# Remainder products of two blocks at once, a one-row bias, one-operation masks and merged placing copies in a gated attention and MLP decode kernel

## The chip, the cores and the metric

The kernel runs on one core of a Trainium2 chip. The metric is the time of one execution on the device, in microseconds, as the median of several runs; the profile is of one further execution, and its span is about 1.2 us shorter than the time of that run. A program on one core can be told apart only as fast or not fast by its distance from the fastest run of the same kernel.

Engines: PE multiplies matrices (PEld is the loading of its weights), DVE is VectorE, ACT is ScalarE, POOL is GpSimd, SP (SyncE) issues nearly all DMA transfers. A load lands when its last bytes have arrived. The granted clock is the share of its full clock that PE was allowed in a stretch of time.

## The reference, cut to what matters

One decode step for 8 sequences: an attention over a sliding window of 2048 positions (32 query heads, 16 key/value heads of 128), a two-layer MLP on a layer norm, and a gate that mixes the two.

```python
x = A_x                                                  # (8, 1, 576)
g = sigmoid((x * gate_w).sum(-1, keepdims=True))
q = x @ wq                                               # 576 -> 32 heads x 128
scores = einsum(q, k[last 2048]) * 128 ** -0.5           # k, v: 8 x 16 x 2048 x 128 bf16 each
a = (softmax(scores) @ v) @ wo                           # 4096 -> 576
b = gelu(layernorm(x) @ w1 + b1) @ w2 + b2               # 576 -> 4608 -> 576
out = g * a + (1 - g) * b
```

K and V are 67 MB each and all weights together 20 MB: 154 MB must come in.

## The kernel before

A small planner lists all operations with their dependences and an assumed cost, orders them for each engine, and puts semaphores in. SP issues the loads in one fixed order. K comes in 16 loads of 4.19 MB into two buffers, V in 32 loads of 2.10 MB into five, which w1 and later w2 share. A load waits, in SP's order, until its buffer is free. Each K unit is transposed twice by DVE and multiplied by PE; after four units two softmaxes follow, and V products use the result.

The parts that the change touches:

```python
# masks, DVE
o_own0 = add("dve", lambda e: e.memset(view("own"), 0.0), ...)
o_own = [add("dve", ... e.memset(own[32*a:32*a+32, a:a+1], 1.0) ...) for a in range(4)]
o_i20 = add("dve", lambda e: e.memset(view("i2"), 0.0), ...)
o_i2 = [add("dve", ... e.tensor_copy(i2[32*q:32*q+32, :, q//2, :], ident[block q]) ...) for q in range(4)]
for q in range(4):
    o_i32.append(add("dve", ... e.tensor_copy(i32[32*q:32*q+32, :], ident[block q]) ...))
...
# wq: 576 rows are 4 x 128 and a remainder of 64; two halves of the columns share the 128 rows of wq_r
for hq in range(Hq):                                     # 32 blocks of 128 columns
    out_ = ps[:, BK_Q, hq*8: hq*8+8]
    for t in range(4):
        e.matmul(out_, wq_m[:, t, block hq], xT[:, t, :], start=(t == 0), stop=False)
    c = hq % 16
    e.matmul(out_, wq_r[:, block c], xT[:, 4 + hq//16, :], start=False, stop=True)
...  # w1 the same: 36 blocks of 4 + 1 products, weights read with a step of 9 columns
# softmax of a group, DVE: the maxima of three row groups copied beside the first's, then
m01 = max(MX, GA); m23 = max(GB_, GC_); tt = max(m01, m23)
...
# placing: quadrant copies of the attention output into the layout that wo's products want
if i == NUQ - 9:
    place(slice(0, 8), slice(0, 6), list(oT_done.values()))
elif i >= NUQ - 8:                                       # after each two of the last eight V units
    c = (i % 8) // 2
    place_done[c] = place(slice(c, 8, 4), slice(6, 8), [oT_done[i-1], oT_done[i]])   # 16 copies
...
# bias of the second layer, loaded into 8 rows, multiplied by 1 - g on the diagonal
d = dma("sp", lambda e: e.dma_start(b2_sb, B_b2.partition_broadcast(8)), ...)
# the loads: each waits for its buffer, in SP's order
d = dma("sp", load, "s%d" % s, 32*512*Dh*2, deps=slot_free[s] + slot_free[s+1], after=last_dma[-1:])
```

## Time and profile before

| | before |
|---|---|
| time, median (three runs) | 366.19 us (366.12 to 366.73) |
| span of the profiled run | 364.9 us |
| DMA | 154.58 MB, 424 GB/s over the span, 90% or more busy in 39 of 40 slices |
| PE, DVE busy | 239.4 us (66%), 226.5 us (62%) |
| end of the last load to the end of the span | 362.2 to 364.9 us |

The page's slices and the chain of waits are shown in the prediction. First the chain's shares by engine, on which rival 1 of the prediction rests:

```profile
DMA 62%; DVE 24%; PE 11%; issue 1%; SPq 0%; DVEq 0%
```

Second the timeline (start us, length us, engine and line, what, count) where wq's products run, one L474 product per group of five being a remainder:

```profile
18.34 0.25 PE L472 MATMUL ps<-arena 128*128 128x8 bf16 x4
18.45 0.17 PE L474 MATMUL ps<-arena 128*128 128x8 bf16 x1
```

Third the timeline near the end: the last V unit's products (L711), the last 16 placing copies (L761), and two of PE's waits for pieces of w2.

```profile
350.07 1.90 PE L711 MATMUL ps<-arena 128*32 128x512 bf16 x16 [1.11 <-DMA arena<-in_A_v_cache_dram]
...
354.06 3.03 DVE L761 COPY arena<-arena 32x4 bf16<-32x4 bf16 x16
...
359.39 1.64 PE L555 MATMUL ps<-arena 128*8 128x288 bf16 x24 [1.35 <-DMA arena<-in_B_w_dram]
361.52 0.53 PE L555 MATMUL ps<-arena 128*8 128x288 bf16 x6 [0.49 <-DMA arena<-in_B_w_dram]
```

The brackets give the idle time of the engine just before, and what ended it. PE stands waiting for w2 at the end.

### The profile page before, as it was taken

What the parts mean: (1) busy time and instruction counts of PE and PEld (TensorE: products, weight loads), DVE (VectorE), ACT (ScalarE), POOL (GpSimd) and SP (SyncE); (2) the same over time, 40 slices, a digit from 0 to 9 for tenths busy, and PEclk for the clock granted to TensorE, in tenths of its full rate; (3) what the DMA queues carried; (4) which work ended last, traced back from release to release, by engine and by line L of the source; (5) the groups of instructions that cost most, each with busy time, mean ns of one, the idle gap of its engine ahead of it and who ended that gap; (6) DMA issues with size and microseconds to landing.
All of it is one profiled execution on the core that took longest, in us unless ns stands there. A gap on an engine that the chain in (4) does not pass through costs nothing.

```text
span 364.9 us, 3980 instructions
## 1 busy us (share of the span) xinstructions
PE 239.4 (66%) x1679; PEld 115.0 (32%) x1679; DVE 226.5 (62%) x340; ACT 22.4 (6%) x53; POOL 17.4 (5%) x80
## 2 busy tenths in 40 slices
PE   0269684838498938274959484738959297577575
PEld 0159331312143414022423232214424133234232
DVE  4700995675999280759965362789781739777221
ACT  1010000000000000000100000001100000001000
POOL 5021000001000000010000000000000000000000
PEclk9999998778589969596996978676978796859899
DMA  9999999999999999999999999999999999999995
GB/s 376 435 404 451 406 451 411 451 432 415 445 426 443 420 436 431 424 438 424 436 426 440 422 442 420 439 422 438 424 436 444 426 410 436 425 431 429 431 425 222
DMA packets 9690, 154.58 MB, mean 424 GB/s; under 512 B 1052, under 2 KB 1220, under 8 KB 2888
## 3 DMA queue, kind: packets, MB, share of 16 engines
q1 hardware_dynamic: 9616, 154.29, 98.9%
q8 instruction: 13, 0.21, 0.2%
q10 hardware_dynamic: 56, 0.03, 0.0%
q14 instruction: 5, 0.04, 0.0%
HBM read 154.31 MB, written 0.01 MB: 423 GB/s over the span
## 4 chain that ended last, share of the span: by engine, by line
DMA 62%; DVE 24%; PE 11%; issue 1%; SPq 0%; DVEq 0%
DMA arena<-in_A_k_cache_dram 54%; DVE arena L666 18%; PE ps L678 6%; DMA arena<-in_A_v_cache_dram 5%; PE ps L711 4%; DMA arena<-in_B_w_dram 4%; DVE arena L639 3%; DVE arena L597 1%; DVE arena L631 1%; DVE arena L600 0%; DVE arena L606 0%; PE ps L612 0%; DVE arena L614 0%; PE ps L555 0%; SPq L798 0%
## 5 line engine op out<-in xcount | busy, mean ns | idle before, releaser
L666 DVE STREAM_TRANSPOSE arena<-arena 128x4096 f32<-128x4096 f32 x32 | 140.7, 4424 | 85.4 <-DMA arena<-in_A_k_cache_dram 85.0
L678 PE MATMUL ps<-arena 128*32 128x512 bf16 x512 | 141.7, 440 | 62.7 <-DVE arena L666 62.7
L678 PEld LDWEIGHTS ps<-arena 128*32 128x32 bf16 x512 | 52.3, 105 | 144.7 <-DVE arena L666 67.7
L711 PE MATMUL ps<-arena 128*32 128x512 bf16 x512 | 60.7, 453 | 23.8 <-DVE arena L602 18.6
L711 PEld LDWEIGHTS ps<-arena 128*32 128x32 bf16 x512 | 24.8, 110 | 50.4 <-issue 31.7
L639 DVE STREAM_TRANSPOSE arena<-arena 128x512 bf16<-128x512 bf16 x32 | 30.8, 1019 | 0.0
L728 PE MATMUL ps<-arena 128*128 128x16 f32 x128 | 17.0, 264 | 5.6 <-ACT arena L722 3.9
L761 DVE COPY arena<-arena 32x4 bf16<-32x4 bf16 (+1 forms) x80 | 12.9, 161 | 10.1 <-POOL arena L749 7.9
L728 PEld LDWEIGHTS ps<-arena 128*128 128x128 f32 x128 | 15.5, 191 | 11.5 <-ACT arena L722 9.6
L722 ACT ACTIVATE arena<-ps 128x512 f32<-128x512 f32 x16 | 9.6, 598 | 148.9 <-PE ps L711 148.9
L749 POOL TENSOR_TENSOR arena<-arena 128x8 bf16<-128x8 f32 x30 | 5.9, 231 | 229.9 <-ACT arena L738 229.9
L597 DVE TENSOR_REDUCE arena<-ps 128x1 f32<-128x512 f32 x8 | 5.5, 692 | 12.2 <-PE ps L678 12.1
L510 PE MATMUL ps<-arena 128*128 128x8 bf16 x144 | 10.9, 201 | 2.6 <-DMA arena<-in_B_w_dram 2.6
L608 ACT ACTIVATE arena<-ps,arena 128x512 bf16<-128x512 f32 x8 | 5.5, 687 | 107.4 <-DVE arena L606 107.4
L510 PEld LDWEIGHTS ps<-arena 128*128 128x128 bf16 x144 | 10.8, 157 | 3.1 <-DMA arena<-in_B_w_dram 3.1
L555 PE MATMUL ps<-arena 128*8 128x288 bf16 (+1 forms) x140 | 9.3, 288 | 3.6 <-DMA arena<-in_B_w_dram 3.4
L659 POOL TENSOR_TENSOR arena<-arena 128x32 bf16<-128x32 bf16 x32 | 6.5, 240 | 86.0 <-PE ps L678 76.9
L612 PE MATMUL ps<-arena 128*128 128x32 f32 x16 | 3.9, 328 | 8.6 <-DVE arena L611 8.6
L631 DVE TENSOR_SCALAR arena<-arena 128x512 bf16<-128x512 bf16 x32 | 9.0, 324 | 0.0
L425 PE MATMUL ps<-arena 8*128 8x8 bf16 x8 | 0.6, 170 | 11.0 <-DVE arena L398 7.0
L512 PE MATMUL ps<-arena 128*128 128x8 bf16 x36 | 7.2, 201 | 0.0
L555 PEld LDWEIGHTS ps<-arena 128*8 128x8 bf16 (+1 forms) x140 | 4.6, 85 | 7.8 <-DMA arena<-in_B_w_dram 4.9
(84 smaller groups left out, 77.8 us busy)
## 6 DMA issues: line engine op xcount, KB each, us to landing
arena<-in_A_k_cache_dram SPq DMA_DIRECT2D x16, 4096.0 KB, 25.2
arena<-in_A_v_cache_dram SPq DMA_DIRECT2D x32, 2048.0 KB, 24.3
arena<-in_B_w_dram SPq DMA_DIRECT2D x1, 4608.0 KB, 24.1
arena<-in_A_wo_dram SPq DMA_DIRECT2D x4, 1152.0 KB, 10.0
arena<-in_A_wq_dram SPq DMA_DIRECT2D x1, 4096.0 KB, 13.4
arena<-in_B_w_dram SPq DMA_DIRECT2D x3, 1296.0 KB, 18.9
arena<-in_B_w_dram SPq DMA_DIRECT2D x2, 432.0 KB, 12.2
arena<-in_B_w_dram SPq DMA_DIRECT2D x1, 576.0 KB, 25.2
```

The lines of the kernel that those rows point to most:

```text
L510: ins = e.matmul(out_, lhsT, yT[:, kt, :], start=(kt == 0), stop=False)
L512: ins = e.matmul(out_, lhsT, yT[:, 4 + c // 2, :], start=False, stop=True)
L555: ins = e.matmul(ps[c:c + 8, BK_ACC, 0:JN], lhsT, rhs[:, JN * j:JN * j + JN], start=False, stop=True, skip_group_check=True, tile_position ...
L597: mx = add("dve", lambda e: e.tensor_reduce(out=k(MX), in_=ps[:, bank, :], axis=AXL.X, op=ALU.max), deps=[qk_done[g]], name="mx%d" % g, co ...
L631: return e.tensor_scalar(out=dst, in0=view("Pd").rearrange("p (s n) -> p s n", s=2), scalar1=amask[:, a:a + 1], scalar2=None, op0=ALU.mult)
L639: return e.transpose(dst, src)
L666: tr = add("dve", (lambda h=h, kb=kb: lambda e: e.transpose(bass.AP(arena_f, offset=foffs("KT") + kb * SE // 2, ap=[[AST // 2, 128], [4, 1 ...
L678: mm = e.matmul(ps[32 * c:32 * c + 32, 2 * (G % 2) + nb, :], qb[:, G % 2, n, 2 * h + ee, :], rhs, start=(h == 0 and t == 0), stop=(h == 1 ...
L711: mm = e.matmul(ps[c:c + 32, bk, :], PT[:, g % 2, 512 * q + 32 * t:512 * q + 32 * t + 32], slot(s)[:, 512 * t:512 * t + 512], start=(t < 2 ...
L722: u_ev[item] = add("act", lambda e: e.activation(out=EV[:, item % 2, :], in_=ps[:, bk, :].rearrange("p (r d j) -> p r j d", r=4, j=4), fun ...
L728: mm = e.matmul(ps[:, BK_S, OC + 16 * (item % 2):OC + 16 * (item % 2) + 16], EV[:, item % 2, 128 * r:128 * r + 128], i2[:, r, :, :].rearra ...
L761: return [add("dve", (lambda j=j, q=q: lambda e: e.tensor_copy(oT[32 * q:32 * q + 32, ch, j, bs], oN[32 * j:32 * j + 32, q, ch, bs]))(), d ...
```

## The change

Its intent is fewer instructions. The two column halves of wq_r share their 128 rows, so one product with 16 columns serves a block of each half; w1 alike. Masks come from one reduction over the identity each. Three maxima become one reduction over four neighbouring columns. The placing copies of the first three pairs of the last eight V units are merged, so they wait for the third pair. The bias is loaded as one row. A small buffer (o32) gets a slice for each item, so its writer no longer waits.

```diff
-        o_own0 = ...memset 0; o_own = four memsets
+        o_own = [add("dve", lambda e: e.tensor_reduce(out=view("own"), in_=ident "p (a i) -> p a i", axis=AXL.X, op=ALU.max), ...)]
-        o_i20 = ...memset 0; o_i2 = four copies; o_i32 = four copies
+        o_i2 = two tensor_reduce;  o_i32 = one tensor_reduce
...
-            for hq in range(Hq):
-                for t in range(4):
-                    ins = e.matmul(out_, wq_m[:, t, ...], xT[:, t, :], start=(t == 0), stop=False)
-                ins = e.matmul(out_, wq_r[:, c * 128:(c + 1) * 128], xT[:, 4 + hq // 16, :], start=False, stop=True)
+            for c in range(Hq // 2):
+                both = ps[:, BK_Q, 0:Hq * 8].rearrange("p (s c b) -> p c s b", s=2, b=8)[:, c, :, :]
+                e.matmul(both, wq_r[:, c * 128:(c + 1) * 128], xT[:, 4:6, :], start=True, stop=False, ...)
+                for hq in (c, c + Hq // 2):
+                    for t in range(4):
+                        ins = e.matmul(ps[:, BK_Q, hq * 8: hq * 8 + 8], wq_m[:, t, ...], xT[:, t, :], start=False, stop=(t == 3), ...)
...  (w1 in the same way)
-            m01 = ...; m23 = ...; tt = ...
+            tt = add("dve", lambda e: e.tensor_reduce(out=k(TT, 1, 32), in_=k(MX, 4, 32), axis=AXL.X, op=ALU.max), deps=sh, ...)
...
-                elif i >= NUQ - 8:
-                    c = (i % 8) // 2
-                    place_done[c] = place(slice(c, 8, 4), slice(6, 8), [oT_done[i - 1], oT_done[i]])
+                elif i == NUQ - 3:
+                    place_done.append(place(0, 3, slice(6, 8), [oT_done[t] for t in range(NUQ - 8, NUQ - 2)]))
+                elif i == NUQ - 1:
+                    place_done.append(place(3, 4, slice(6, 8), [oT_done[i - 1], oT_done[i]]))
...
-            d = dma("sp", lambda e: e.dma_start(b2_sb, B_b2.partition_broadcast(8)), ...)
+            d = dma("sp", lambda e: e.dma_start(b2_sb, B_b2.partition_broadcast(1)), ...)
```

More of the change, by code (lines that the diff above doesn't have):

```diff
@@ L171 @@
 ARENA_BASE = 16512
-def held_matmul(nc, e, out, lhsT, rhs, start=False, stop=True, skip=False, tile_size=(128, 128), tile_position=(0, 0)):
-    return e.add_instruction(mybir.InstMatmult(
-        name=nc.get_next_instruction_name(), engine=mybir.EngineType.PE,
-        ins=[e.lower_ap(rhs), e.lower_ap(lhsT)], outs=[e.lower_ap(out)],
-        start_tensor_calc=start, stop_tensor_calc=stop, is_transpose=False, bass_skip_group_check=skip,
-        tile_size=tile_size, tile_position=tile_position, ldweights=False))
 def build_kernel(nc, A_x, A_k_cache, A_v_cache, A_wq, A_wo, B_x, B_w1, B_b1, B_w2, B_b2, gate_w, out):
@@ L246, in build_kernel @@
         req("rg", 2 * 32, F32)
-        req("o32", 2 * 16, F32)
+        req("o32", (Hkv - 1) * 16, F32)
         req("EV", 2 * 512, F32)
@@ L304, in build_kernel @@
         b1T = view("b1T")
-        b2_sb = view("b2", 8)
+        b2_sb = view("b2", 1)
         u_sb, uh_sb, v1_sb, v2_sb = view("u"), view("uh"), view("v1"), view("v2")
         hT = view("hT").rearrange("p (t b) -> p t b", b=8)
-        ob = view("ob", 8)
-        ot32 = view("ot32", 8)
+        ob = view("ob", 1)
+        ot32 = view("ot32", 1)
         gb = view("gb")
@@ L314, in build_kernel @@
         rg = view("rg").rearrange("p (g m) -> p g m", g=2)
-        o32 = view("o32").rearrange("p (u m) -> p u m", u=2)
+        o32 = view("o32").rearrange("p (u m) -> p u m", m=16)
         oN = view("oN").rearrange("p (q c b) -> p q c b", q=4, c=8)
@@ L375, in build_kernel @@
             o_selb.append(add("pool", fn, deps=[o_ident], name="selb%d" % he, cost=0.3))
-        o_own0 = add("dve", lambda e: e.memset(view("own"), 0.0), name="own0", cost=0.1)
-        o_own = [add("dve", (lambda a=a: lambda e: e.memset(view("own")[32 * a:32 * a + 32, a:a + 1], 1.0))(), deps=[o_own0], name="own%d" % a, cost=0.1) for a in range(4)]
+        o_own = [add("dve", lambda e: e.tensor_reduce(out=view("own"), in_=ident.rearrange("p (a i) -> p a i", a=4), axis=AXL.X, op=ALU.max), deps=[o_ident], name="own", cost=0.25)]
         o_am = add("dve", lambda e: e.tensor_reduce(out=amask, in_=ident.rearrange("p (q a h) -> p a q h", q=16, a=4), axis=AXL.XY, op=ALU.add), deps=[o_ident], name="amask", cost=0.25)
@@ L453, in build_kernel @@
         o_gb = add("dve", lambda e: e.tensor_copy(gb, ps[:, BK_X, 384:400]), deps=[o_gp], name="gb_ev", cost=0.15)
-        o_obh = add("dve", lambda e: e.tensor_copy(ob[:, 0:8], dg[:, 8:16]), deps=[o_dgb], name="ob_hi", cost=0.12)
+        o_obh = add("dve", lambda e: e.tensor_copy(ob[:, 0:8], gb[0:1, 8:16]), deps=[o_gb], name="ob_hi", cost=0.12)
         o_ob32 = add("dve", lambda e: e.tensor_copy(ot32, ob[:, 0:8]), deps=[o_obh], name="ob_32", cost=0.12)
-        o_obl = add("dve", lambda e: e.tensor_tensor(out=ob[:, 8:16], in0=dg[:, 8:16], in1=ot32, op=ALU.subtract), deps=[o_ob32], name="ob_lo", cost=0.12)
+        o_obl = add("dve", lambda e: e.tensor_tensor(out=ob[:, 8:16], in0=gb[0:1, 8:16], in1=ot32, op=ALU.subtract), deps=[o_ob32], name="ob_lo", cost=0.12)
@@ L458, in build_kernel @@
         o_i32 = []
-        o_i20 = add("dve", lambda e: e.memset(view("i2"), 0.0), name="i2z", cost=0.1, prio=-1)
-        o_i2 = [add("dve", (lambda q=q: lambda e: e.tensor_copy(i2[32 * q:32 * q + 32, :, q // 2, :], ident[32 * q:32 * q + 32, 32 * q:32 * q + 32].rearrange("p (r m) -> p r m", r=4)))(),
-                    deps=[o_i20, o_ident], name="i2_%d" % q, cost=0.15, prio=-1) for q in range(4)]
-        for q in range(4):
-            o_i32.append(add("dve", (lambda q=q: lambda e: e.tensor_copy(i32[32 * q:32 * q + 32, :], ident[32 * q:32 * q + 32, 32 * q:32 * q + 32]))(),
-                             deps=[o_ident, o_obl], name="i32_%d" % q, cost=0.15, prio=-1))
+        o_i2 = [add("dve", (lambda u=u: lambda e: e.tensor_reduce(out=i2[:, :, u, :], in_=ident[:, 64 * u:64 * u + 64].rearrange("p (a r m) -> p r m a", a=2, r=4), axis=AXL.X, op=ALU.max))(),
+                    deps=[o_ident], name="i2_%d" % u, cost=0.2, prio=-1) for u in range(2)]
@@ L467, in q_fn @@
+        o_i32.append(add("dve", lambda e: e.tensor_reduce(out=i32, in_=ident.rearrange("p (a m) -> p m a", a=4), axis=AXL.X, op=ALU.max), deps=[o_ident, o_obl], name="i32", cost=0.25, prio=-1))
         def q_fn(e):
             ins = None
-            for hq in range(Hq):
-                out_ = ps[:, BK_Q, hq * 8: hq * 8 + 8]
-                for t in range(4):
-                    ins = e.matmul(out_, wq_m[:, t, hq * 128:(hq + 1) * 128], xT[:, t, :], start=(t == 0), stop=False)
-                c = hq % 16
-                ins = e.matmul(out_, wq_r[:, c * 128:(c + 1) * 128], xT[:, 4 + hq // 16, :], start=False, stop=True)
+            for c in range(Hq // 2):
+                both = ps[:, BK_Q, 0:Hq * 8].rearrange("p (s c b) -> p c s b", s=2, b=8)[:, c, :, :]
+                e.matmul(both, wq_r[:, c * 128:(c + 1) * 128], xT[:, 4:6, :], start=True, stop=False, skip_group_check=True)
+                for hq in (c, c + Hq // 2):
+                    for t in range(4):
+                        ins = e.matmul(ps[:, BK_Q, hq * 8: hq * 8 + 8], wq_m[:, t, hq * 128:(hq + 1) * 128], xT[:, t, :], start=False, stop=(t == 3), skip_group_check=True)
@@ L496, in build_kernel @@
         o_q4 = add("act", q4_fn, deps=[o_selp], name="q4_ev", cost=1.2)
-        H_CH = 6
+        H_CH = 3
         o_hch = []
-        for i0 in range(0, FT, H_CH):
-            fts = list(range(i0, min(FT, i0 + H_CH)))
+        for i0 in range(0, FT // 2, H_CH):
+            fts = list(range(i0, i0 + H_CH))
             def fn(e, fts=fts):
@@ L506, in fn @@
                     c, j = divmod(t, FJ)
-                    out_ = ps[:, BK_H, t * 8: t * 8 + 8]
-                    for kt in range(4):
-                        lhsT = bass.AP(arena, offset=aoffs("RAW") + W1O + kt * F + FCW * c + j, ap=[[AST, 128], [FJ, 128]])
-                        ins = e.matmul(out_, lhsT, yT[:, kt, :], start=(kt == 0), stop=False)
-                    lhsT = bass.AP(arena, offset=aoffs("RAW") + W1O + 4 * F + FCW * (c % 2) + j, ap=[[AST, 128], [FJ, 128]])
-                    ins = e.matmul(out_, lhsT, yT[:, 4 + c // 2, :], start=False, stop=True)
+                    both = ps[:, BK_H, 0:FT * 8].rearrange("p (s t b) -> p t s b", s=2, b=8)[:, t, :, :]
+                    lhsT = bass.AP(arena, offset=aoffs("RAW") + W1O + 4 * F + FCW * c + j, ap=[[AST, 128], [FJ, 128]])
+                    e.matmul(both, lhsT, yT[:, 4:6, :], start=True, stop=False, skip_group_check=True)
+                    for s in range(2):
+                        for kt in range(4):
+                            lhsT = bass.AP(arena, offset=aoffs("RAW") + W1O + kt * F + FCW * (c + 2 * s) + j, ap=[[AST, 128], [FJ, 128]])
+                            at = (t + s * FT // 2) * 8
+                            ins = e.matmul(ps[:, BK_H, at: at + 8], lhsT, yT[:, kt, :], start=False, stop=(kt == 3), skip_group_check=True)
                 return ins
-            o_hch.append(add("pe", fn, deps=dw1 + [o_yT], name="h_pe%d" % len(o_hch), cost=0.06 * 5 * len(fts), after=o_hch[-1:]))
+            o_hch.append(add("pe", fn, deps=dw1 + [o_yT], name="h_pe%d" % len(o_hch), cost=0.06 * 9 * len(fts), after=o_hch[-1:]))
         o_hp = o_hch[-1]
@@ L594, in softmax @@
             k = lambda i, n=1, parts=128, p0=0: sm[p0:p0 + parts, g, i:i + n]
-            MX, GA, GB_, GC_, M01, M23, TT, NB, S = range(9)
+            MX, GA, GB_, GC_, TT, NB, S = range(7)
             bank = g % 4
@@ L600, in softmax @@
                 sh.append(add("dve", (lambda i=i, dst=dst: lambda e: e.tensor_copy(k(dst, 1, 32), k(MX, 1, 32, 32 * i)))(), deps=[mx], name="mg%d_%d" % (g, i), cost=0.16, prio=5))
-            m01 = add("dve", lambda e: e.tensor_tensor(out=k(M01, 1, 32), in0=k(MX, 1, 32), in1=k(GA, 1, 32), op=ALU.max), deps=[sh[0]], name="m01_%d" % g, cost=0.16, prio=5)
-            m23 = add("dve", lambda e: e.tensor_tensor(out=k(M23, 1, 32), in0=k(GB_, 1, 32), in1=k(GC_, 1, 32), op=ALU.max), deps=sh[1:], name="m23_%d" % g, cost=0.16, prio=5)
-            tt = add("dve", lambda e: e.tensor_tensor(out=k(TT, 1, 32), in0=k(M01, 1, 32), in1=k(M23, 1, 32), op=ALU.max), deps=[m01, m23], name="t_%d" % g, cost=0.16, prio=5)
+            tt = add("dve", lambda e: e.tensor_reduce(out=k(TT, 1, 32), in_=k(MX, 4, 32), axis=AXL.X, op=ALU.max), deps=sh, name="t_%d" % g, cost=0.16, prio=5)
             nbs = []
@@ L737, in v_compute @@
                 if item < Hkv - 1:
-                    ev = add("act", lambda e: e.activation(out=o32[:, item % 2, :], in_=osrc, func=ACTF.Copy), deps=[prev] + ([oT_done[2 * item - 4], oT_done[2 * item - 3]] if item >= 2 else []), name="oev%d" % item, cost=0.25, prio=3)
+                    ev = add("act", lambda e: e.activation(out=o32[:, item, :], in_=osrc, func=ACTF.Copy), deps=[prev], name="oev%d" % item, cost=0.25, prio=3)
                     o_item_ev[item] = ev
                     b6_r.append(ev)
-                    eng, src_, deps = "pool", o32[:, item % 2, :], [ev, rg_done[g]]
+                    eng, src_, deps = "pool", o32[:, item, :], [ev, rg_done[g]]
                 else:
@@ L752, in v_compute, with place @@
                 if i == NUQ - 9:
-                    place(slice(0, 8), slice(0, 6), list(oT_done.values()))
-                elif i >= NUQ - 8:
-                    c = (i % 8) // 2
-                    place_done[c] = place(slice(c, 8, 4), slice(6, 8), [oT_done[i - 1], oT_done[i]])
-        place_done = {}
-        def place(ch, bs, deps):
-            return [add("dve", (lambda j=j, q=q: lambda e: e.tensor_copy(oT[32 * q:32 * q + 32, ch, j, bs], oN[32 * j:32 * j + 32, q, ch, bs]))(), deps=deps, name="pl%d%d" % (j, q), cost=0.1, prio=2)
-                    for j in range(4) for q in range(4)]
+                    place(0, 4, slice(0, 6), list(oT_done.values()))
+                elif i == NUQ - 3:
+                    place_done.append(place(0, 3, slice(6, 8), [oT_done[t] for t in range(NUQ - 8, NUQ - 2)]))
+                elif i == NUQ - 1:
+                    place_done.append(place(3, 4, slice(6, 8), [oT_done[i - 1], oT_done[i]]))
+        place_done = []
+        def place(c0, c1, bs, deps):
+            ops = []
+            for j in range(4):
+                for q in range(4):
+                    dst = oT[32 * q:32 * q + 32, :, j, bs].rearrange("p (a c) b -> p a c b", a=2)[:, :, c0:c1, :]
+                    src = oN[32 * j:32 * j + 32, q, :, bs].rearrange("p (a c) b -> p a c b", a=2)[:, :, c0:c1, :]
+                    ops.append(add("dve", (lambda dst=dst, src=src: lambda e: e.tensor_copy(dst, src))(), deps=deps, name="pl%d%d" % (j, q), cost=0.1, prio=2))
+            return ops
         def wo_chunk(i):
@@ L780, in project @@
                         ds.append(d)
-                AccGroup("proj%d" % c, mms, place_done[c] + ds, cost=1.1)
+                AccGroup("proj%d" % c, mms, place_done[c // 3] + ds, cost=1.1)
         o_m2, o_ac = [], []
         def bias(i):
-            d = dma("sp", lambda e: e.dma_start(b2_sb, B_b2.partition_broadcast(8)), "b2", 65536, name="d_b2", after=last_dma[-1:])
+            d = dma("sp", lambda e: e.dma_start(b2_sb, B_b2.partition_broadcast(1)), "b2", 65536, name="d_b2", after=last_dma[-1:])
             last_dma.append(d)
```

## The prediction

> **What bounds the kernel now.** I began with the page's head and slices: which engine is full, and is it full everywhere?
>
> ```profile
> span 364.9 us, 3980 instructions
> ...
> PE 239.4 (66%) x1679; PEld 115.0 (32%) x1679; DVE 226.5 (62%) x340; ACT 22.4 (6%) x53; POOL 17.4 (5%) x80
> ...
> DMA  9999999999999999999999999999999999999995
> ...
> DMA packets 9690, 154.58 MB, mean 424 GB/s; under 512 B 1052, under 2 KB 1220, under 8 KB 2888
> ...
> q1 hardware_dynamic: 9616, 154.29, 98.9%
> q8 instruction: 13, 0.21, 0.2%
> ```
>
> The reader is to see that PE and DVE are two thirds busy, while the transfers are at 90% or more in 39 slices of 40; only the last slice, where the kernel winds up, has less. Nearly all bytes (154.29 of 154.58 MB) come through one queue, the loads that SyncE issues.
>
> Second, the chain of waits, its last pieces (start us, length us, what):
>
> ```profile
> 345.21 2.74 PE ps L711 x12
> ...
> 348.51 0.33 SPq L798
> ...
> 349.35 12.86 DMA arena<-in_B_w_dram
> 362.21 0.04 issue
> 362.26 0.67 PE ps L555 x6
> 362.93 0.02 issue
> 362.95 0.45 DVE arena L826
> ```
>
> The end is the last piece of w2 landing at 362.21, six small products, one addition, and the store: 364.9 - 362.2 = 2.7 us after the last load. The chain also names DVE for 24% and PE for 11%. That is misleading: it goes back through whoever released the buffer of a load, but a load issued late delays nothing if others are still queued ahead of it. So, third, the time from issue to landing of the K loads and of the V loads, taken for each tensor by itself:
>
> ```profile
> DMA to landing us min/median/max: 15.0/25.2/34.3
> ...
> DMA to landing us min/median/max: 13.6/24.3/34.4
> ```
>
> First line K (16 loads of 4.19 MB), second V (32 of 2.10 MB). The loads take from about 1.2 us (the first work, after the program's first issues) to 362.2 us, so they move 154.29 MB / 361 us = 427 GB/s. One K load needs 9.8 us of that, one V load 4.9. Even the quickest K load spent 15.0 - 9.8 = 5.2 us on other things, and the quickest V load 13.6 - 4.9 = 8.7 us, mostly behind earlier loads. The queue is never near empty. Hence the sum: 1.2 us head + 361 us of transfer + 2.7 us tail = 364.9. Only a change of bytes, of the rate, of the head or of the tail moves it.
>
> Fourth, the last microseconds, stretch by stretch (the last two columns are the DMA share and GB/s):
>
> ```profile
> 359.00:360.00 1.00, 0.61 (x10) 0.45 (x12) 0.00 (x0) 0.00 (x0) 0.00 (x0) 1.00 0.98 378
> 360.00:361.00 1.00, 1.00 (x18) 0.50 (x12) 0.00 (x0) 0.00 (x0) 0.00 (x0) 1.00 0.54 207
> 361.00:362.00 1.00, 0.51 (x8) 0.18 (x6) 0.00 (x0) 0.00 (x0) 0.00 (x0) 1.00 0.38 138
> ```
>
> The share falls through 0.54 and 0.38 instead of stopping at once: the 16 DMA engines don't finish together, and the last one sets the landing.
>
> [...] (the rate is 0.9 or more in slices where DVE is at 9 and where it is at 0), so less DVE work should not speed the loads. [...] a product with 16 columns should cost what one with 8 does. The trace has 8-column products of wq every 26.7 ns (below), and no 16-column bf16 ones. [...] The placing copies agree, 160 ns for 4 elements a partition and 167 for 48:
>
> ```profile
> L761 DVE COPY arena<-arena 32x4 bf16<-32x4 bf16 x64 | 10.2, 160 | 9.9 <-POOL arena L749 7.9
> L460 DVE CAST arena<-arena 32x32 f32<-32x32 bf16 x4 | 3.5, 875 | 0.1
> L761 DVE COPY arena<-arena 32x48 bf16<-32x48 bf16 x16 | 2.7, 167 | 0.2
> ```
>
> **The change part by part.**
>
> *Remainder products.* wq: 32 blocks of 4 + 1 products become 16 groups of 1 + 8, 160 to 144. In the timeline, groups of five follow each other every 0.133 us (18.32, 18.45, 18.58), 26.7 ns a product, so 16 x 26.7 ns = 0.43 us. w1: 180 to 162; groups start every 0.30 us (27.25, 27.55), 60 ns a product, so 18 x 60 ns = 1.08 us. Both are off the path. wq's end at 22.5 us releases the second K load, which then queues behind w1 and the first K load (landed at 36.6 us). w1's products end near 37.7 us, and the next products wait for the first K transpose (done 41.1 us) anyway.
>
> *Masks.* Ownership: five memsets of 0.06 us become one reduction; a similar one (128x4 from 128x128) took 0.29 us, so nothing. The i2 pattern: one memset and four casts, 0.11 + 4 x 0.875 = 3.6 us, become two reductions of half that reduction's input, about 0.2 us each by estimate from it: 3.2 us less DVE. They end at 5.9 us, and DVE then stands idle 4.15 us until gate_w lands at 10.07. i32: four casts spanning 0.78 us become one, some 0.3 us: 0.5 us, in the shadow of the loads. All zero on the path.
>
> *Softmax maxima.* Per group, three maxima (126, 140, 147 ns) become one reduction over four columns, about 0.15 us: 0.27 us x 8 = 2.1 us less DVE. K transposes and K issues come earlier by as much, into a queue with at least 5.2 us before it: zero.
>
> *Placing.* 64 small copies become 32: 32 x 160 ns = 5.1 us less busy, about 6 us elapsed (a block of 16 spans 3.03 us). But the three earlier blocks now start together, after the sixth of the last eight units, near 344.6 us, and end near 347.7. The first two projections move from 336.5 and 338.0 us to behind that: 32 products, about 1.3 us at 0.66 us for 16, plus 0.66 for the third. They end near 350, where the last V load arrives (350.07). In the changed order the product that frees the last w2 buffer (345.2 to 348.5 us) stands ahead of the projections, so the last w2 issue isn't delayed. PE waits 1.35 us for w2 at 356.3 and again at 359.4, enough for a small slip. The fourth block stays, 354.06 to 357.1.
>
> *Bias as one row.* 8 packets of 1152 B become one row: 8.06 KB less, 8.06 / 427 GB/s = 0.02 us on average; on the engine that ends last at most one packet, 0.05 us in the record of packets.
>
> *Program size.* 34 products (each a load and a multiply in the trace) and 58 DVE operations go (4 + 3 + 3 + 16 + 32): 126 of 3980, 3%. Instruction fetches are 0.21 MB, so 0.5 us spread over all engines, and 3% of that is 0.02 us.
>
> Sum: about -0.1 us on the path, against some 12 us less work on engines that are not. 366.19 - 0.1 = 366.1 us.
>
> **The rivals.** (1) *The released work counts*: if the chain's 24% of DVE and 11% of PE were real delays, the 3.2 + 0.5 + 2.1 + 5.1 us of DVE and 1.5 us of PE would give up to 3% together, 354 to 360 us. For it speaks only the chain; against it, the full slices and the 5.2 us of queue. (2) *The late projections delay the end*: PE sits between the last V unit and w2, and its granted clock was 0.50 from 345 to 348 us. At half clock the moved products take perhaps 2.5 us in place of 1.3, and the last V product slips by 1 to 2 us. If w2's products were to pile up behind, the end would slip by that, 367 to 368 us; the waits at 356.3 and 359.4 speak against it. (3) *Which DMA engine ends last*: 13 instruction fetches of 16 KB occupy single engines; one takes 16.4 KB / (427/16 GB/s) = 0.6 us of one engine. If the smaller program drops a fetch, or moves one to or from the last engine, the end moves by up to 0.6 us either way. This is the largest uncertainty that I hold real. [...]
>
> **Range and chances.** Before's three runs span 0.6 us, and rival 3 is 0.6 us, so 366.1 with 365.3 to 366.9. Two per cent is 7.3 us: only rival 1 in full gets there, 1%; slower takes a new stall of the queue, 1%; within 2%, 98%.
>
> **What would show it.** Right: the DMA row again at 9 in 39 slices, K and V landing times within a few us of these, the last w2 landing within 1 us of 362.2, the same six products and addition after it; DVE busy lower by some 11 us and PE by 1 to 2, both as more idle time. The wq group should take 9 x 26.7 = 0.24 us, showing 16 columns free. Wrong: a landing several us earlier (rival 1), or a wait at the end for projections or placing copies (rival 2).

Measured: 427 GB/s on average while loads run (single slices up to 451), and a DMA share of 0.9 or more in slices with DVE at 9 tenths and in slices with DVE at 0. That 16 columns cost what 8 do was, when it was written, an assumption; the changed kernel bore it out (26.7 ns a product, below). The 160 and 167 ns of the placing copies stand as measured. The sum: 1.2 + 361 + 2.7 = 364.9 us of span as it was, about 0.1 us less for the bias (0.02 to 0.05 us) and the shorter program (0.02 us), so 366.19 - 0.1 = 366.1 us of time.

## The result, and the profile after

| | before | after |
|---|---|---|
| time, median of the runs taken together | 366.15 us (4 runs) | 366.24 us (4 runs, 366.04 to 366.39) |
| ratio of fast runs, after over before | | 0.9999 (95%: 0.9981 to 1.0016) |
| span of the profiled run | 364.9 us | 365.1 us |

A ratio here is the mean time of one kernel's fast runs over that of the other's of the same rounds, so it isn't quite the ratio of the medians quoted. The two kernels take the same time. The page of the changed kernel:

```profile
span 365.1 us, 3841 instructions
...
PE 239.9 (66%) x1645; PEld 113.4 (31%) x1645; DVE 216.8 (59%) x282; ACT 22.3 (6%) x53; POOL 17.4 (5%) x80
...
DMA  9999999999999999999999999999999999999995
...
q8 instruction: 13, 0.21, 0.2%
...
DMA 54%; DVE 29%; PE 14%; issue 2%; SPq 0%; ACT 0%; DVEq 0%
```

DVE is 9.7 us less busy (226.5 to 216.8) with 58 instructions fewer, PE has 34 products fewer, and the DMA row is the same, digit for digit. The load queue went from 9616 to 9602 packets: 7 fewer of 1152 B (136 to 129) and 7 fewer of 4 B (1024 to 1017), which fits the bias as eight rows of one packet each becoming one. The chain (last line) nevertheless gives DVE 29% in place of 24%. The last pieces of the chain of waits, and the time from issue to landing of the K loads (first line) and the V loads:

```profile
348.43 13.93 DMA arena<-in_B_w_dram
...
362.40 0.68 PE ps L545 x6
...
363.10 0.45 DVE arena L820
```

```profile
DMA to landing us min/median/max: 15.1/25.2/34.5
...
DMA to landing us min/median/max: 14.2/24.0/34.7
```

The last piece of w2 landed at 348.43 + 13.93 = 362.36 us, against 362.21 before; after it come the same six products and the same addition. The last stretches (DMA share and GB/s in the last two columns):

```profile
359.00:360.00 1.00, 0.94 (x24) 0.63 (x26) 0.01 (x1) 0.22 (x1) 0.00 (x0) 1.00 0.94 370
360.00:361.00 1.00, 1.00 (x20) 0.62 (x16) 0.00 (x0) 0.19 (x1) 0.00 (x0) 1.00 0.59 232
361.00:362.00 1.00, 0.50 (x10) 0.18 (x6) 0.00 (x0) 0.00 (x0) 0.00 (x0) 1.00 0.37 133
```

They fall off as before. The wq products in the timeline, one 16-column remainder (L459) and eight others (L462):

```profile
18.15 0.17 PE L459 MATMUL ps<-arena 128*128 128x16 bf16 x1
18.18 0.35 PE L462 MATMUL ps<-arena 128*128 128x8 bf16 x8
...
18.39 0.17 PE L459 MATMUL ps<-arena 128*128 128x16 bf16 x1
```

Nine products in 18.39 - 18.15 = 0.24 us, 26.7 ns each, as before: the second block of columns is free here. And the end of PE's work:

```profile
350.58 2.00 PE L699 MATMUL ps<-arena 128*32 128x512 bf16 x10
...
355.97 3.04 DVE L755 COPY arena<-arena 32x4 bf16<-32x4 bf16 x16
...
359.06 2.15 PE L545 MATMUL ps<-arena 128*8 128x288 bf16 x40 [0.90 <-DVE arena L755]
361.71 0.54 PE L545 MATMUL ps<-arena 128*8 128x288 bf16 x6 [0.50 <-DMA arena<-in_B_w_dram]
```

Here something did move: the last placing copies start 1.9 us later than before (355.97 against 354.06). At 359.06 us PE now waits 0.90 us for these copies; the prediction had named such a wait as a sign of being wrong. But PE then still waits 0.50 us for w2, so the wait for the copies does not reach the end.

### The profile page after: what moved, and what is told of

Read it like the earlier page. It is cut to its first block, busy times and chain, and to the rows that moved or that the text cites. A ratio compares the mean times of both kernels' runs of the same rounds, so it can differ in the third digit from the quotient of the medians.

```text
span 365.1 us, 3841 instructions
## 1 busy us (share of the span) xinstructions
PE 239.9 (66%) x1645; PEld 113.4 (31%) x1645; DVE 216.8 (59%) x282; ACT 22.3 (6%) x53; POOL 17.4 (5%) x80
## 3 DMA queue, kind: packets, MB, share of 16 engines
q1 hardware_dynamic: 9602, 154.28, 98.9%
## 4 chain that ended last, share of the span: by engine, by line
DMA 54%; DVE 29%; PE 14%; issue 2%; SPq 0%; ACT 0%; DVEq 0%
DMA arena<-in_A_k_cache_dram 46%; DVE arena L654 20%; PE ps L666 9%; DVE arena L627 5%; DMA arena<-in_A_v_cache_dram 4%; PE ps L699 4%; DMA arena<-in_B_w_dram 4%; DVE arena L587 1%; DVE arena L619 1%; DVE arena L590 1%; DVE arena L594 1%; DVE arena L602 0%; PE ps L716 0%; DVE arena L599 0%; SPq L792 0%
## 5 line engine op out<-in xcount | busy, mean ns | idle before, releaser
L666 PE MATMUL ps<-arena 128*32 128x512 bf16 x512 | 142.7, 442 | 63.8 <-DVE arena L654 63.8
L699 PE MATMUL ps<-arena 128*32 128x512 bf16 x512 | 62.2, 460 | 23.9 <-DVE arena L627 18.9
L716 PEld LDWEIGHTS ps<-arena 128*128 128x128 f32 x128 | 15.5, 191 | 11.5 <-ACT arena L710 9.6
L755 DVE COPY arena<-arena 32x48 bf16<-32x48 bf16 (+2 forms) x48 | 7.9, 164 | 17.6 <-POOL arena L737 16.4
L502 PE MATMUL ps<-arena 128*128 128x8 bf16 x144 | 9.8, 201 | 0.0
L502 PEld LDWEIGHTS ps<-arena 128*128 128x128 bf16 x144 | 9.8, 158 | 0.0
L600 PEld LDWEIGHTS ps<-arena 128*128 128x128 f32 x16 | 2.6, 203 | 11.2 <-DVE arena L599 9.1
```

Source lines behind the costliest of these rows:

```text
L502: ins = e.matmul(ps[:, BK_H, at: at + 8], lhsT, yT[:, kt, :], start=False, stop=(kt == 3), skip_group_check=True)
L666: mm = e.matmul(ps[32 * c:32 * c + 32, 2 * (G % 2) + nb, :], qb[:, G % 2, n, 2 * h + ee, :], rhs, start=(h == 0 and t == 0), stop=(h == 1 ...
L699: mm = e.matmul(ps[c:c + 32, bk, :], PT[:, g % 2, 512 * q + 32 * t:512 * q + 32 * t + 32], slot(s)[:, 512 * t:512 * t + 512], start=(t < 2 ...
L716: mm = e.matmul(ps[:, BK_S, OC + 16 * (item % 2):OC + 16 * (item % 2) + 16], EV[:, item % 2, 128 * r:128 * r + 128], i2[:, r, :, :].rearra ...
L755: ops.append(add("dve", (lambda dst=dst, src=src: lambda e: e.tensor_copy(dst, src))(), deps=deps, name="pl%d%d" % (j, q), cost=0.1, prio=2))
```

## The experiments

Two theories. "Loads": the time is head + bytes / rate + tail, and what the change took off PE and DVE lay beside loads. "Released work counts": the chain gives DVE 24% and PE 11%, so work on them should show. All kernels passed the comparison with the reference. Each was compared with runs of the kernel before on the same chip in the same rounds; their median was 366.3 to 366.4 us throughout.

### The removed work, done twice (removed_twice)

The kernel before with the removed work added once more:

```diff
 # each wq block and each w1 block
+                e.matmul(out_, wq_m[:, 0, block hq], xT[:, 0, :], start=True, stop=True)     # overwritten by the next
 # own, i2, i32: written twice;  softmax:
+            for again in range(2):
+                m23 = add("dve", ... max(GB_, GC_) ..., deps=[m23])
 # placing, the first two blocks
+                    first = place(...) if c < 2 else []
```

> The kernel before, with the work that the change removes done twice over (right result): one product more for each of the 32 wq blocks (26.7 ns each) and 36 w1 blocks (60 ns each), about 3.0 us of PE; the masks, two more maxima a group and the first two placing blocks again, about 11.8 us of DVE. Theory 'loads': every one of these lies in time in which the queue of loads is not empty, so 366.2 us, within 0.6, with DVE busy near 238 us and PE busy 1 to 3 us higher. Theory 'released work counts': DVE has 24% of the chain of waits and PE 11%, so a quarter of the added work or all of it shows, +3 to +15 us.

Measured: 366.25 us, ratio 0.9993 (0.9981 to 1.0006).

```profile
PE 243.5 (67%) x1747; PEld 118.4 (32%) x1747; DVE 235.3 (64%) x400; ACT 22.4 (6%) x53; POOL 17.4 (5%) x80
```

PE rose by 4.1 us (1 to 3 expected) and DVE by 8.8 us (less than the 11.8 expected: the second four i2 casts ran faster than the first, 481 ns on average over all eight), and nothing came of it. Work of this amount at these places costs nothing when added, so it should give nothing when removed. (The one-row bias and the o32 slices are not in this run; only the comparison of the two kernels covers them.) "Released work counts" expected at least 3 us.

### Four V loads halved (half_v)

The changed kernel, with half of four V units left at what the buffer held before, so wrong (the comparison with the reference, with its tolerance, passed all the same):

```diff
+            if 8 <= i < 12:
+                src = ...the same rows, half as long...
+                dst = slot(s)[:, 0:SE // 2]
```

> The changed kernel with the load of four of the 32 V units halved (wrong result on purpose; the other half of the buffer keeps old data, all compute stays): 4.19 MB less. Theory 'loads': the time follows the bytes, 4.19 MB at 427 GB/s = 9.8 us less, 356.4 us, within 1. Theory 'released work counts': V loads hold 4 to 5% of the chain of waits, and no compute is removed, so less than 2 us.

Measured: 356.57 us, ratio 0.9731 (0.9716 to 0.9746).

```profile
q1 hardware_dynamic: 9602, 150.09, 98.8%
...
339.25 13.20 DMA arena<-in_B_w_dram
```

4.19 MB less on the queue (154.28 to 150.09), the last landing at 339.25 + 13.20 = 352.45 us, and 366.37 - 356.57 = 9.8 us less time: 4.19 MB / 9.8 us = 428 GB/s. No instruction was taken away. These bytes count in full.

### How much delay the queue absorbs (dve_plus4, dve_plus8, dve_plus4s, dve_plus2)

The changed kernel with one idle reduction on DVE between the landing of every K load and its transposes, so that all K buffers come free later:

```diff
+            tr_hist.append(add("dve", lambda e: e.tensor_reduce(out=(an unused cell), in_=(the ones, 12 times 320), axis=AXL.XY, op=ALU.max),
+                               deps=[d, o_ones], cost=4.0, after=tr_hist[-1:]))
```

> The changed kernel with one reduction of 3840 elements (about 4.0 us) on DVE between the landing of each of the 16 K loads and its transposes, so that every K buffer comes free 4 us later: 64 us more DVE work, 217 to 281 us busy. Theory 'loads': DVE was busy some 157 of the 240 us in the middle, and the quickest K load stood behind 5.2 us of others, so the queue still doesn't run empty: 366.2 to 367.5 us, with the shortest time from issue to landing of K some 4 us lower. Theory 'released work counts': at DVE's 24 to 29% of the chain, +15 to +19 us.

> The same with 8.0 us in place of 4.0: 128 us more DVE work. Theory 'loads': now DVE becomes the bound, since four K units take 78.5 us of loads and would take 51 + 32 = 83 us of DVE, and from the first landed K (36.6 us) about 328 us of DVE work follow before the last unit's probabilities are done, 35 us later than now: 385 to 402 us, with gaps in the DMA row. Theory 'released work counts': about twice the loss at 4.0 us.

The first pair told the planner the true cost, and it reordered PE. So two more were run with cost 0.0, which keeps the other engines' orders as in the changed kernel:

> The same with 3840 elements (4.15 us), as in the earlier run, but with the order of every other engine kept. If the loss of 10.2 us came from the delay itself, 376 us within 2; if it came from the order that the planner chose for PE, 366 to 370 us. The DMA row must show below 9 in the same slices in the first case.

> The changed kernel with one reduction of 1920 elements (about 2.1 us) on DVE between the landing of each of the 16 K loads and its transposes: 33 us more DVE work, with every other engine's order kept as in the changed kernel (in the run with 4.0 us the planner had also reordered PE). That run lost 10.2 us of its 64, in four places where the queue of loads ran dry. Theory 'a reserve in the queue': delays are free until the reserve is used up; half the delay leaves most of those places filled: 366.2 to 368 us, less than a quarter of the loss at 4.0. Theory 'released work counts at a fixed share': half the loss, 371.3 us.

| run | DVE busy, against 216.8 us | time, median | ratio to before (95%) |
|---|---|---|---|
| dve_plus2 | +32 us | 369.07 us | 1.0078 (1.0058 to 1.0097) |
| dve_plus4s | +64 us | 376.08 us | 1.0253 (1.0227 to 1.0279) |
| dve_plus4, PE reordered | +64 us | 376.38 us | 1.0267 (1.0253 to 1.0281) |
| dve_plus8, PE reordered | +127 us | 414.98 us | 1.1324 (1.1309 to 1.134) |

The DMA row of dve_plus4s:

```profile
DMA  9999989999997899999999999999999979999995
GB/s 393 426 417 445 410 325 414 446 426 426 447 412 337 327 419 447 417 443 421 445 421 384 417 445 417 450 415 439 428 426 421 428 315 430 420 440 428 434 421 241
```

Holes appear where the row was full: 325, 337, 327 and 315 GB/s in slices that had some 410 to 450. dve_plus4s and dve_plus4 agree in the loss, so it is the delay and not PE's order. The expectations were missed in part. At 4 us a unit "loads" had allowed 1.3 us, and dve_plus4 lost 10.0; "released work counts" had 15 to 19. At 8 us the time was 414.98 us, neither the 385 to 402 of "loads" nor twice the loss at 4 us. And dve_plus2 lost 2.8 us, more than the 0 to 2 us expected and 30% of the loss at twice the delay, where a fixed share would give 50%. The loss grows faster than the work: 0.09 us per added us for the first 32 us, 0.2 for the next 32, then 0.6 (with PE reordered).

So there is a reserve, but a small one. My 5.2 us was not all reserve. The time from issue to landing of the K loads in dve_plus8, where the queue does run empty:

```profile
DMA to landing us min/median/max: 12.9/16.0/34.4
```

A K load issued there at 54.18 us, 2.96 us after the load before it had landed, took 13.0 us, whereas behind a full queue a K load lands 9.7 us after the load before it. So 3.3 of the 5.2 us were no reserve, and about 2 us are left. The times of single loads in the traces agree. The K load with the least ahead of it in the changed kernel was issued at 45.88 us, 5.5 us before the load ahead of it landed. In dve_plus2 it was issued 1.9 us later and landed no later (60.73 against 61.03 us); in dve_plus4s it was issued 3.8 us later and landed 1.7 us later. Delays of units also add up: the K load issued at 111.94 us in the changed kernel was issued 3.8 us later in dve_plus2, and 10.4 us later in dve_plus4s, where the queue was empty by then; it added 0.7 and 4.9 us to the lateness of the landings. The rest of dve_plus2's loss in its profile (1.7 us in all) arose at loads with 13 us or more ahead of them, and stays unexplained. Its six runs lie in two clumps (367.9 to 368.5 and 369.6 to 370.2 us); the profile is of the lower one.

### The placing in four blocks again (place_by_block)

```diff
-                elif i == NUQ - 3:
-                    place_done.append(place(0, 3, slice(6, 8), [...six units...]))
-                elif i == NUQ - 1:
-                    place_done.append(place(3, 4, ...))
+                elif i >= NUQ - 8:
+                    c = (i % 8) // 2
+                    place_done.append(place(c, c + 1, slice(6, 8), [oT_done[i - 1], oT_done[i]]))
```

> The changed kernel with the last placing copies in four blocks, each as soon as its own two units are ready, as before (right result). In the changed kernel the first three blocks start together at 346.4 us, the last V unit's products fall into a stretch at half clock, and the last block starts at 355.97 us, 1.9 us later than before (354.06). Theory 'loads': the time stays 366.2 us within 0.4, but the last block starts near 354.1 us again and PE again waits for w2 (over 1 us) before the last products. Rival 'late projections': if the merged placing had cost time that another part of the change gave back, this one is faster by 0.5 to 2 us.

Measured: 366.71 us, ratio 1.0005 (0.9993 to 1.0017).

```profile
350.07 3.53 PE L699 MATMUL ps<-arena 128*32 128x512 bf16 x16 [0.82 <-DMA arena<-in_A_v_cache_dram]
...
355.69 3.03 DVE L754 COPY arena<-arena 32x4 bf16<-32x4 bf16 x16
```

The ratio shows no difference from the kernel before (the median is 0.1 us above the expected range), so the merging costs nothing and gains nothing that these runs show. But the copies start at 355.69 us, not near 354.1: the last V unit's products start on time (350.07, as before) and take 3.53 us in place of 1.90, in a stretch where the granted clock averaged 0.57. In the changed kernel it was 0.56 from 350.5 to 354 us; before, 1.00 from 350 to 354 us. PE's last two waits for w2 were 0.43 and 0.47 us, not over 1 us as expected. So the 1.9 us shift goes with where the clock was low in these profiles; the merging can't be its only cause, and I had ascribed it to the merging. From 350 to 354 us the clock was 0.57 to 0.62 in the profiles of the changed kernel, place_by_block, tail4_after and tail4s_after, but 1.00 in more_code and in the four with the order of the kernel before (before, removed_twice, tail4_before, tail4s_before). What in the change, if anything, moves the low stretch there was not tested.

### Delaying the last copies (tail4_after, tail4_before, tail4s_after, tail4s_before)

In both kernels, just ahead of the last 16 placing copies:

```diff
+                    add("dve", lambda e: e.tensor_reduce(out=(an unused cell), in_=(the ones, 12 times 320), ...),
+                        deps=[o_ones, oT_done[i - 1], oT_done[i]], cost=4.0, prio=9)     # cost=0.0 in the pair with s
```

> The changed kernel with one reduction of about 4.15 us on DVE just ahead of its last block of placing copies. Theory 'the merged placing spent slack': the last block ended 359.0 us, 40 products of 2.15 us follow it, and PE then waited only 0.50 us for w2; so of 4.15 us all but about 0.5 to 1.4 show: +2.8 us, 369.0 us, within 0.8. Theory 'the tail hides anything': no change, 366.2 us.

> The kernel before with the same reduction of about 4.15 us just ahead of its last block of placing copies, which there began 1.9 us earlier (354.06 us): the last block would end at 361.3 us, 40 products of 2.15 us and 12 of about 0.55 us follow, 364.0 us in place of 362.95 us: +1.0 us, 367.2 us, within 0.8, and 1.9 us less than the changed kernel with the same addition loses. If both lose the same, the changed order cost no slack.

Measured: 367.51 us (1.0026, 1.0013 to 1.0038) and 367.40 us (1.0031, 1.0019 to 1.0043). The first was expected at 369.0, the second at 367.2 us. Inconclusive for the question: told of the cost, the planner had put the last projection behind pieces of w2, so that PE had other work meanwhile. Again with PE's order kept:

> The changed kernel with one reduction of about 4.15 us on DVE just ahead of its last block of placing copies, now with the order of PE kept (in the earlier pair the planner had moved the last projection behind pieces of w2, which hid part of it). Theory 'the merged placing spent slack': last block to 363.2 us, then 40 products of 2.15 us and 12 of 0.55 us, the last addition at 365.9 instead of 363.1 us: 369.0 us, within 0.8. Theory 'the tail hides it': 366.2 us.

> The kernel before with the same addition and PE's order kept: last block to 361.3 us, 40 products and 12 products, the last addition at 364.0 instead of 362.95 us: 367.3 us, within 0.8, so some 1.7 us less loss than the changed kernel. If both lose the same, the changed order cost no slack.

Measured: 371.03 us (1.0114, 1.0096 to 1.0133) and 370.87 us (1.0112, 1.0095 to 1.0129). Both lose the same, so the theory that the changed order has less slack at its end falls; by these runs it has no less. Both lost more than expected, because the last 52 products took longer than I had worked out. The stretch from their start to their end, changed kernel first (the third number from the end is the granted clock):

```profile
362.90:367.80 4.90, 4.83 (x52) 2.54 (x52) 0.01 (x1) 0.41 (x1) 0.00 (x0) 0.58 0.02 3
```

```profile
361.10:366.40 5.30, 5.22 (x52) 2.77 (x52) 0.04 (x1) 0.41 (x1) 0.00 (x0) 0.54 0.06 23
```

52 products took 4.8 to 5.2 us at a granted clock of 0.54 to 0.58; I had put 2.7 us, from profiles in which the clock was 1.00 there. Both sets of five runs lie in two clumps (369.3 to 369.8 and 370.9 to 371.4 us); I didn't find out what separates them. The two profiles come one from each clump (371.03 and 369.59 us), so the 1.8 us between the starts of their 52 products says nothing of the two kernels.

### More instructions (more_code)

The changed kernel with 22 small products ahead of each of the first 24 V units:

```diff
+                for t in range(22 if i < 24 else 0):
+                    e.matmul(ps[:, BK_ACC, 320:328], ident, ident[:, 0:8], start=False, stop=True, ...)
```

> The changed kernel with 22 more 8-column products (into columns that nobody reads) ahead of each of the first 24 V units: 528 products, 1056 PE instructions, 14 us of PE at 26.7 ns each, none near the end. Theory 'instruction fetches share the DMA engines' (rival 3 of the prediction): the fetches go from 13 to about 17 packets of 16 KB, each 0.6 us of one engine, so the end moves by 0.1 to 1.2 us, and the DMA rows show the fetches. Rival: fetches are hidden, 366.2 us within 0.3. In neither do the 14 us of PE count.

Measured: 367.69 us, ratio 1.0039 (1.0027 to 1.0051), 1.4 us more, a little over the range.

```profile
q8 instruction: 17, 0.28, 0.3%
...
361.00:362.00 1.00, 0.57 (x10) 0.22 (x6) 0.00 (x0) 0.00 (x0) 0.00 (x0) 1.00 0.52 196
362.00:363.00 1.00, 0.00 (x0) 0.00 (x0) 0.00 (x0) 0.00 (x0) 0.00 (x0) 1.00 0.23 70
```

Four more packets of instructions, as expected (17 of 16 KB for 4897 instructions, 13 for 3841), and a longer fall-off at the end. The trace records every DMA packet with its start and length. The last piece of w2 puts eight packets of 1152 B on each of the 16 engines, one every 47 ns, so the 16 trains can be told apart, and with them when each engine finished (us from the first packet of the load queue):

```
               first    mean of 16   last
before         358.36   359.90       361.17
after          358.56   359.85       361.32
more_code      358.43   360.30       362.82
```

The first engine ends within 0.2 us of the same time in all three; the last one, which sets the landing, is 1.5 us later with more code. In four more profiles with 13 packets (removed_twice, place_by_block, tail4_after, tail4_before) the last engine ended at 361.10 to 361.55. In bytes, four packets of 16 KB are 0.15 us over all engines, and the loss is ten times that. The packets show where part of it arose. The train that ends last in more_code sends nothing from 360.61 to 361.11 us, then a packet of 374 ns where others of its size take 135, and is held up by some 1.0 us in all. The last fetch of instructions runs from 360.14 to 361.13 us. So one fetch on the engine that ends last fits most of the 1.5 us. The record doesn't name the engines, so this is argued from the times, not shown; and the other programs have a last fetch near there too (358.90 us before, 360.06 after). Why only more_code's meets the engine that ends last stays open. Nor is it excluded that the added products themselves, PE being 21 us busier, shifted something else, though the queue has no hole.

## Why the prediction was right

The prediction was 366.1 us, 365.3 to 366.9, with 98% for no change. Measured were 366.24 us and a ratio of 0.9999.

- *What bounds the kernel: the loads.* Shown. The half-loads followed the bytes at 428 GB/s (the prediction had 427), with no instruction removed.
- *The removed work lies beside loads.* Shown in the other direction: doing it twice changed nothing. The kernel's DVE busy time fell by 9.7 us; the prediction had 11.
- *The chain's 24% of DVE isn't a cost (rival 1).* Shown for the size of this change. It isn't true for any size: 32 us more at the K loads cost 2.8 us, 64 cost 9.8 to 10.0. The share itself says little: it rose to 29% when DVE had 9.7 us less to do.
- *A queue of at least 5.2 us.* The conclusion held, the number didn't. The K load with the least ahead of it has a reserve of about 2 us: the prediction took only the 9.8 us of transfer off the 15.0 us, but a K load with nothing ahead of it took 13.0. Delays of several units also add up. A change that made DVE slower by 4 us a unit would have been predicted wrong.
- *16 columns cost as much as 8.* Shown for wq: 0.24 us for nine products, 26.7 ns each at a granted clock of 1.00, with one of 16 columns among them. For w1 the groups of nine follow each other every 0.54 us, 60 ns each, as predicted, also at 1.00. w1's weights are read with a step of 9 columns and wq's are packed, and the means of their weight loads are 158 and 104 ns; the runs don't isolate the step as the cause.
- *Rival 2, the late projections.* The slip of the last V unit came, 1.9 us, and was absorbed before the end, as held likelier. But the margin was smaller than thought: in place of the two waits of 1.35 us for w2 that the prediction counted on, PE waited 0.90 us for the copies and 0.50 us for w2. The merged blocks started at 346.44 us, not near 344.6. The cause of the slip was not the merged copies alone: with separate blocks the same products were slow too.
- *PE busy 1 to 2 us lower.* Wrong in sign: 239.4 to 239.9 us, with 34 products fewer. The V products' mean rose from 453 to 460 ns and the K products' from 440 to 442 ns, 1.5 and 1.0 us in sum, which hides the saving; the low-clock stretches fall elsewhere (granted clock, before and after: 0.70 and 1.00 from 345 to 350 us, 1.00 and 0.72 from 350 to 356 us).
- *Rival 3, the engine that ends last.* Held as the largest uncertainty; in this pair it didn't matter, since both programs fetched 13 packets (the smaller program has 139 instructions fewer, not 126). The added code moved the end by 1.4 us with four packets more, which supports that such packets can do so. The 0.6 us for one packet on one engine was too low: the fetches are recorded at 0.88 to 0.99 us (spread over all 16 engines, 16.4 KB at 427 GB/s would take 0.04 us, so a fetch does seem to hold one engine).

No version that beats both came out of the experiments: at the measured 428 GB/s the 154 MB alone take some 360 of the 365 us, so nothing off the loads can gain much here.

## What to carry to other kernels

Before counting what a change saves, ask whether the transfers ever stop. Here the DMA row was full in 39 of 40 slices. 4.19 MB less gave 9.8 us, while 8.8 us more DVE work and 4.1 us more PE work cost nothing, and the chain of waits, with 24% for DVE, overstated an engine that merely released buffers. Test it both ways, by doubling the work in question and by dropping bytes. Don't read the queue's reserve off the time to landing alone: take off what a load needs with nothing ahead of it (13.0 us for a K load here, where its share of the rate was 9.8), and remember that delays of several loads added up here. A reserve that hid some 10 us of scattered work did not hide 32 us put at the K loads.
